# z2 of a gated MLP by one level of Strassen on blocks of 256 columns, on one NeuronCore

## The chip, the core and the metric

The kernel runs on one core of a Trainium2 chip. The metric is device time in microseconds (us) of one execution. The engines are PE (TensorE, matmuls), DVE (VectorE), ACT (ScalarE), POOL (GpSimd) and SP (SyncE, which here issues every DMA).

## The reference, cut to what matters

```python
xn = _layernorm(x)                                   # x: 2048 tokens x 576
s  = A(xn)                                           # sliding-window attention, 32 heads of 18, then @ wo
z  = _gelu(xn @ w_in)                                # 2048 x 4608
z1, z2 = z[..., :2304], _layernorm(z[..., 2304:])
g  = einsum("ts,bsf->btf", w_sp, z2) + b_sp[None, :, None]     # w_sp: 2048 x 2048
out = x + s * _silu((z1 * g) @ w_out)
```

The change is in the product `xn @ w_in[:, 2304:]`, called the z2 projection: 2048 x 576 times 576 x 2304, with gelu and the statistics of the layer norm behind it. All matrix products are done in fp32 by splitting each operand into a high part (fp32r) and a low part: three matmuls, high x high, high x low and low x high.

## The kernel before

The stages follow one another: statistics and transposes of x with the q/k projection, the values projection, the z2 projection, attention with the z1 projection filling its gaps, the output projection of attention, the product with w_sp (by Strassen with seven products, from sums of its quarters that were written to DRAM earlier), and the product with w_out (also by Strassen).

From the first stage on, the normalised x lies transposed in SBUF as 18 planes (`plane`, L192): nine groups of 64 inputs, high parts in planes 0 to 8, low parts in 9 to 17. A plane is 128 partitions by 1024 columns; partitions 0 to 63 hold one half of the tokens, 64 to 127 the other. A matmul on the upper and one on the lower 64 rows (`h` = 0, 1) run as a pair on PE; `steps_on` (L204) issues 27 such pairs for one token tile of 128 per half: nine planes by three matmuls.

The values stage (L942 to L957) makes two halves of 288 columns by eight token tiles `q`; each tile is evicted by ACT into `ve` and stored to v_d.

The z2 stage (L965 to L1002) makes six pieces of 384 columns by eight token tiles. For each tile: 27 pairs, gelu from PSUM by ACT (L991), `bn_stats` by DVE (L992), and after every second tile a store to z2_d (L994). The weights of the next piece are fetched by SP and halved by ACT and DVE (`split`, L117) meanwhile (`load_z2`, L906). In the last piece the first heads of attention are loaded (`pair_jobs`, L539) and 32 score maxima are put between the matmuls (`max_item`, L606).

Beside the z2 stage, `sp_combos` (L864) makes the sums of w_sp's quarters that the product with w_sp needs later: 16 rounds, each of four loads of 128x512 (256 KB), four GpSimd sums and four stores to sc_d. It is a generator: after each token tile the loop calls `next(combos)` once (L983), and a round takes three of these calls. Its four tiles a11, a12, a21, a22 come from the pool `wc` with `WCB` = 2 buffers each, and a round's loads are issued before the stores of the round before.

In this part of the kernel the order of the instructions of each engine, SP included, is the program's order (`manual_schedule`). SP waits for what a DMA needs (data to be stored, or a buffer whose earlier users, stores among them, are done) before it goes on to the next DMA. PSUM has eight banks; `pair_banks` gives the projections two pairs of them in turn.

## Time and profile before

| | us |
|---|---|
| median of three runs | 1827.39 (1827.34 to 1832.03) |
| the profiled execution | 1826.5 |
| its span, first to last instruction | 1824.4 |

A profile shows one execution. Its page has busy times by engine, the chain of work that ended last, and the costliest groups of instructions by line; windows give the same by stretches of time, and a timeline gives single instructions with what they waited for. Times are us from the start of the span unless marked ns. L209 is line 209 of the kernel before. A matmul's listed duration is its latency; matmuls overlap, so the distance between the starts of two of them tells the rate.

### The profile page before, as it was taken

Reading aid. Unit: us, or ns where it says so; the run is one execution under the profiler, and the core shown is the slowest. Engines: PE = TensorE matmul, PEld = TensorE weight load, DVE = VectorE, ACT = ScalarE, POOL = GpSimd, SP = SyncE. Lnnn points to the kernel's source line nnn. Section 1 sums busy time; section 2 is a strip of 40 time slices with the busy share of each in tenths; the row PEclk is TensorE's granted clock in tenths of the full one; section 3 lists DMA queues with packets and bytes.
Section 4 is the critical chain, followed back from the end, with each engine's and each line's share of the span. In section 5 each row is a group of like instructions: output and inputs, shape, how many; then the busy total and the mean of one; then the engine's idle time right before and its main releaser. Section 6 shows DMA issues by size and latency. Waiting matters only on the chain.

```text
span 1824.4 us, 37719 instructions
## 1 busy us (share of the span) xinstructions
PE 1798.9 (99%) x14373; PEld 1589.3 (87%) x14373; DVE 1129.3 (62%) x2314; ACT 931.9 (51%) x1742; POOL 427.7 (23%) x507
## 2 busy tenths in 40 slices
PE   8999999999999999999999999999999999999998
PEld 8999999998887887886988888888888888899998
DVE  7321333457676776671257687677876667767876
ACT  5433222222766666766467665466454534444443
POOL 3332333343455655645000000113000000000000
PEclk9999999999999999999999999999999999999999
DMA  8895688887567777765877768798786556797554
GB/s 275 194 231 168 226 278 283 279 269 240 162 167 205 197 185 195 202 166 167 266 236 251 236 214 282 242 300 298 233 284 233 178 176 200 255 264 205 159 156 137
DMA packets 266918, 405.73 MB, mean 222 GB/s; under 512 B 52337, under 2 KB 180593, under 8 KB 266609
## 3 DMA queue, kind: packets, MB, share of 16 engines
q1 hardware_dynamic: 266736, 403.32, 72.3%
q8 instruction: 113, 1.85, 0.4%
q14 instruction: 69, 0.56, 0.1%
HBM read 285.35 MB, written 117.09 MB: 221 GB/s over the span
## 4 chain that ended last, share of the span: by engine, by line
PE 83%; DMA 7%; DVE 5%; ACT 2%; SPq 2%; issue 1%; POOL 0%; ACTq 0%; DVEq 0%; POOLq 0%
PE acc L1498 35%; PE mb L209 11%; PE c L1590 8%; PE ma L209 5%; PE s L696 5%; PE ops L784 4%; PE t L696 3%; PE wops L1217 3%; PE ma L696 2%; PE mb L696 1%; SPq L366 1%; PE s L619 1%; DMA wraw<-in_w_qk_dram 1%; PE s L755 1%; DMA st_d<-qkhl 1%
## 5 line engine op out<-in xcount | busy, mean ns | idle before, releaser
L1498 PE MATMUL acc<-spl,zh 128*128 128x512 f32 x1008 | 392.6, 390 | 0.9 <-DVE spl L119 0.6
L1498 PE MATMUL acc<-sph,zl 128*128 128x512 f32 x1008 | 392.2, 389 | 0.0
L1498 PE MATMUL acc<-sph,zh 128*128 128x512 f32 x1008 | 392.2, 389 | 0.0
L119 DVE TENSOR_TENSOR spl<-spr,sph 128x1024 fp32r<-128x1024 f32 x168 | 210.3, 1252 | 39.5 <-ACT sph L118 37.9
L1498 PEld LDWEIGHTS acc<-spl,zh 128*128 128x128 f32 x1008 | 189.2, 188 | 41.7 <-DVE spl L119 2.6
L1498 PEld LDWEIGHTS acc<-sph,zh 128*128 128x128 f32 x1008 | 189.2, 188 | 39.4
L1498 PEld LDWEIGHTS acc<-sph,zl 128*128 128x128 f32 x1008 | 189.2, 188 | 39.1
L118 ACT ACTIVATE zh<-b 128x384 fp32r<-128x384 f32 x168 | 87.4, 520 | 209.7 <-PE acc L1498 209.4
L118 ACT ACTIVATE sph<-spr 128x1024 fp32r<-128x1024 f32 x168 | 176.0, 1047 | 14.0 <-DMA spr<-in_w_sp_dram 6.4
L119 DVE TENSOR_TENSOR zl<-b,zh 128x384 fp32r<-128x384 f32 x168 | 98.8, 588 | 123.3 <-ACT zh L118 123.2
L623 DVE CUSTOM_DVE_ANT_0 s<-s,band 128x384 f32<-128x384 f32 (+2 forms) x244 | 130.6, 559 | 46.7 <-PE s L619 24.2
L696 PE MATMUL s<-b,z1wh 64*128 64x512 f32 x522 | 155.1, 396 | 0.0
L1590 PE MATMUL c<-b,o 128*128 128x288 f32 x1056 | 144.1, 295 | 1.7 <-DVE o L119 1.7
L1590 PEld LDWEIGHTS c<-b,o 128*128 128x128 f32 x1056 | 141.0, 188 | 2.7 <-DVE o L119 2.4
L759 ACT ACTIVATE pt<-s 128x384 f32<-128x384 f32 (+2 forms) x257 | 111.1, 453 | 43.4 <-PE s L755 30.8
L992 DVE BATCH_NORM_STATS2 st<-zt 128x6 f32<-128x384 f32 x96 | 49.3, 548 | 129.8 <-ACT zt L991 129.4
L696 PE MATMUL t<-b,z1wh 64*128 64x512 f32 x378 | 123.7, 397 | 0.2 <-ACT z1o L706 0.2
L209 PE MATMUL ma<-z2w,b 64*128 64x384 f32 x648 | 116.1, 333 | 0.0
L209 PE MATMUL mb<-z2w,b 64*128 64x384 f32 x648 | 116.0, 333 | 0.0
L209 PE MATMUL ma<-att,b 64*128 64x384 f32 x648 | 112.8, 331 | 0.0
L209 PE MATMUL mb<-att,b 64*128 64x384 f32 x648 | 112.8, 331 | 0.0
L209 PEld LDWEIGHTS mb<-z2w,b 64*128 64x128 f32 x648 | 112.4, 184 | 0.0
(264 smaller groups left out, 4781.9 us busy)
## 6 DMA issues: line engine op xcount, KB each, us to landing
spr<-sc_d SPq DMA_DIRECT2D x96, 512.0 KB
spr<-in_w_sp_dram SPq DMA_DIRECT2D x72, 512.0 KB
zr<-z_d SPq DMA_DIRECT2D x144, 192.0 KB
z_d<-zt SPq DMA_DIRECT2D x48, 384.0 KB
z_d<-z1o SPq DMA_DIRECT2D x72, 256.0 KB
z1t<-z_d SPq DMA_DIRECT2D x72, 256.0 KB
y_d<-z1t SPq DMA_DIRECT2D x72, 256.0 KB
a<-in_w_sp_dram SPq DMA_DIRECT2D x64, 256.0 KB
```

Source lines behind the costliest of these rows:

```text
L118: act.activation(hi, src, AF.Copy)
L119: dve.tensor_tensor(lo, src, f32(hi), ALU.subtract)
L209: pe.matmul(banks[h][:, :n], *both[h][i], start=i == 0, stop=i == STEPS - 1)
L366: sp.dma_start(rows[c].rearrange("i h a p -> (i h) a p"), f32(hl[64 * n:64 * n + 64, c]).rearrange("q (a p) -> q a p", a=2))
L623: dve.tensor_tensor_reduce(out=ps[:, :w], in0=ps[:, :w], in1=band[:, m0:384], scale=1.0, scalar=-3.0e38, op0=ALU.add, op1=ALU.max, accum_o ...
L696: pe.matmul(ps, w, x_, start=n == 0, stop=n == STEPS - 1)
L759: act.activation(pt[:, j, d0:d0 + n * P], ps[:, (qa - a) * P:(qa - a + n) * P], AF.Exp, scale=scale)
L784: pe.matmul(o_ps[c][32 * j:32 * j + 32, (qa - 4 * c) * P:(hi - 4 * c + 1) * P], vgs[u][:, kb - k0, j * VW:j * VW + 32], pt[:, j, (qa - kb) ...
L992: dve.bn_stats(st2[:, s, pc, :], zv)
L1217: pe.matmul(po[:, i, :288], lt[:, cs], r[:, i * 288:(i + 1) * 288], start=n == 0, stop=n == len(pl) - 1)
L1498: pe.matmul(acc[j], z[:, ps], w[:, cs], start=s == i == 0 and n in OPENS, stop=s == 7 and i == 2, skip_group_check=True)
L1590: pe.matmul(banks[key][:, :288], y, w, start=begin and k == n == 0, stop=close and k == 8 and n == 2, skip_group_check=True)
```

## The change

The z2 projection is cut into nine blocks of 256 columns (`ZB`, `NZ`). Eight of them are made in four pairs by one level of Strassen (the form with seven products and shared sums): the tokens in two halves of 512 columns of a plane, the inputs in planes 0 to 3 and 4 to 7, the columns in the two blocks of the pair. Plane 8, the ninth, is no part of the Strassen scheme; its products are added to four of the seven as further steps, with activations from plane 8 itself or the difference of its two token halves (`xdd`). The ninth block is made the plain way.

- The sums of activations (`x_sums`) are made by DVE and ACT during the values stage, one step after each token tile. A fourth operand, the difference of the token halves of planes 0 to 3, is written over the second halves of these planes during the first two products (`third_sum`); what stood there is saved to x_d before and brought back by DMA at the end (`restore`).
- The sums of weights T1 to T4 are made by GpSimd (`form_t`) for each pair of blocks from half blocks that SP fetches (`fetch_w`, `fetch_rem`) during the pair before.
- Each of the seven products is two groups `qq` of two token tiles, into four PSUM banks of its kind; `evict` copies it, adds it to an earlier one, or applies gelu. Finished outputs go through `closed`: gelu, statistics and the store, which are issued after the next group (`run_behind`). The output tiles `zt_tile` come in turn from two pools, seven in all.
- `sp_combos` has one buffer for each tile instead of two, and its loads, sums and stores stand at three successive calls of `next(combos)`. There is one call after each group.
- The head loads stand ahead of the groups of the last pair's fourth to sixth product, the maxima in its seventh and in the ninth block.

The diff, cut to its core:

```diff
-                wc = open_pool(stack, "wc", bufs=WCB)
+                wc = open_pool(stack, "wc", bufs=1)
+                for q, h in ((q, h) for q in range(8) for h in range(2)):
...
+                        sp.dma_start(t, w_sp[i, 8 * j + q, :, cs])
...
                     yield
                     pool.tensor_tensor(a22, a21, a22, ALU.add)
                     pool.tensor_tensor(a21, a11, a21, ALU.subtract)
-                    yield
                     pool.tensor_tensor(a11, a22, a11, ALU.subtract)
                     pool.tensor_tensor(a12, a12, a11, ALU.subtract)
-                    if n + 1 < len(steps):
-                        nxt = load(*steps[n + 1])
                     yield
                     for k, t in enumerate((a22, a11, a21, a12)):
                         sp.dma_start(sc_d[k, q, :, cs], t)
+                    yield
...
+                LEFT = (own(8, 0), own(8, 512), summed(xdd))
+                PARTS = [(own(0, 0), 0, True, None), (own(4, 0), 1, True, (0, 0)), (summed(xs2), 0, False, None),
+                         (summed(xs1), 1, True, (1, 1)), (own(0, 512), 0, False, None),
+                         (own(4, 512), 0, False, (1, 0)), (summed(xs4), 1, False, (2, 1))]
...
+                def x_sums():
...
+                    for i, k0 in ((0, 0), (1, 4)):
+                        sp.dma_start(raw[i], w_z2[0, :, k0:k0 + 4, :])
+                    for i in range(2):
+                        for k in range(4):
+                            sp.dma_start(x_d[i, :, k], f32(half_plane(9 * i + k, 1)))
+                    for k in range(4):
...
+                        dve.tensor_tensor(s, f32(h21), f32(h22), ALU.add)
+                        dve.tensor_tensor(s, s, f32(l21), ALU.add)
+                        dve.tensor_tensor(s, s, f32(l22), ALU.add)
+                        split(xs1[0][:, c], xs1[1][:, c], s)
+                        yield
+                        less(s, h11, l11)
+                        split(xs2[0][:, c], xs2[1][:, c], s)
+                        yield
+                        dve.tensor_tensor(s, f32(h12), s, ALU.subtract)
+                        dve.tensor_tensor(s, s, f32(l12), ALU.add)
+                        split(xs4[0][:, c], xs4[1][:, c], s)
+                        yield
...
-                        if ch == 1 or q >= 6:
-                            next(nxt[1], None)
+                        next(forming, None)
...
+                def fetch_w(key, blk, k0, name):
...
+                    sp.dma_start(t, w_z2[blk, :, k0:k0 + 4, :])
+                def halve_rem(n):
+                    split(rem[:, 0, :n], rem[:, 1, :n], raw_w["rem"][:, :n])
+                def form_t(*names):
+                    b11, b12, b21, b22 = (raw_w[n] for n in ("b11", "b12", "b21", "b22"))
+                    for n in names:
+                        dst, x_, y = {"t3": (b12, b22, b12), "t2": (b11, b12, b11), "t4": (b21, b21, b11),
+                                      "t1": (b11, b22, b11)}[n]
+                        pool.tensor_tensor(dst, x_, y, ALU.add if n == "t2" else ALU.subtract)
+                def group_steps(banks, qq, operands, opens, ends):
+                    for a in range(2):
...
+                        for xo, j, wt in operands:
+                            for xi, wi in ((0, 0), (0, 1), (1, 0)):
+                                for h in range(2):
+                                    pe.matmul(banks[h][:, cs], xo(xi, j, q)[ROWS[h]], wt[ROWS[h], wi],
...
...
+                def evict(n, qq, banks, blks):
+                    for h in range(2):
+                        i, b = 2 * qq + h, banks[h]
+                        if n in (0, 2, 4):
+                            act.activation((u2 if n == 2 else t1)[:, i], b, AF.Copy)
+                        elif n == 1:
+                            zv = zt_tile()
+                            dve.tensor_tensor(zv, b, t1[:, i], ALU.add)
+                        elif n == 5:
+                            zv = zt_tile()
+                            act.activation(zv, b, AF.Gelu_apprx_tanh)
+                        elif n == 6:
+                            zv = zt_tile()
+                            dve.tensor_tensor(zv, b, u2[:, i], ALU.add)
+                        if n == 4:
+                            zv = zt_tile()
+                            dve.tensor_tensor(zv, yb[qq][h], t1[:, i], ALU.add)
...
+                    run_behind()
...
+                for p in range(NP):
...
+                    def prepare(n):
+                        if n == 0:
+                            halve_rem(2)
+                            ops_w[2] = halve(raw_w["b11"])
+                            form_t("t4", "t1")
+                        elif n < 5:
+                            ops_w[n + 2] = halve(raw_w[("b11", "b12", "b21", "b22")[n - 1]])
+                        elif n == 5:
+                            ops_w[7] = halve(raw_w["b11"])
+                        else:
+                            if not final:
+                                form_t("t3", "t2")
+                            ops_w[8] = halve(raw_w["b21"])
+                    def fetches(n):
...
+                        if n == 5 and not final:
+                            fetch_w("b22", nxt + 1, 4, "z1wl")
+                        if n == 6:
+                            fetch_rem((nxt,) if final else (nxt, nxt + 1))
+                    for n, (xo, kind, opens, part_of) in enumerate(PARTS):
...
+                        for qq in range(2):
+                            banks = (xb, yb)[kind][qq]
+                            if qq == 0:
+                                prepare(n)
+                            if final and n > 2:
+                                if qq == 0 and n < 6:
+                                    clear(n - 3)
+                                    heads_in += [job for job in [pair_jobs(n - 3)] for _ in range(8)]
+                                unasked(4)
+                            for m, _ in enumerate(group_steps(banks, qq, operands, opens, n > 4)):
+                                if final and n == 6:
+                                    more_maxima(m)
+                            evict(n, qq, banks, blks)
+                            if qq == 1:
+                                fetches(n)
+                            if p == 0 and n < 2:
+                                third_sum(2 * n + qq)
+                            if final and n in (5, 6):
+                                restore(2 * (n - 5) + qq)
+                            next(combos, None)
...
+                halve_rem(1)
...
+                for qq in range(4):
...
+                    unasked(4)
+                    for m, _ in enumerate(group_steps(banks, qq, operands, True, True)):
+                        more_maxima(m)
+                    next(combos, None)
+                    run_behind()
```

More of the change, by code (lines that the diff above doesn't have):

```diff
@@ L101 @@
     t_d = dram.tile([4, FB, 288], F32, name="t_d")
+    x_d = dram.tile([2, P, 4, 512], F32, name="x_d")
     ident = const.tile([P, P], F32, name="ident")
@@ L874, in load @@
                         ts.append(t)
-                    return ts
-                nxt = load(*steps[0])
-                for n, (q, cs) in enumerate(steps):
-                    a11, a12, a21, a22 = nxt
+                    a11, a12, a21, a22 = ts
                     yield
@@ L932, in token_tile, with difference @@
+                def difference(s, k):
+                    h0, l0, h1, l1 = (half_plane(9 * i + k, t) for t in range(2) for i in range(2))
+                    dve.tensor_tensor(s, f32(h0), f32(h1), ALU.subtract)
+                    dve.tensor_tensor(s, s, f32(l0), ALU.add)
+                    less(s, l1)
+                ops_w = {}
                 def token_tile(q, h):
@@ new lines, in unasked, with more_maxima @@
+                def unasked(n):
+                    for _ in range(n):
+                        if heads_in:
+                            next(heads_in.pop(0), None)
+                def more_maxima(count):
+                    if count % 6 == 3 and ahead:
+                        max_item(0, *ahead.pop(0))
+                fetch_w("b11", 0, 0, "z1wh")
+                fetch_w("b12", 1, 0, "z1wl")
+                fetch_w("b22", 1, 4, "z1wl")
+                fetch_w("b21", 0, 4, "z1wh")
+                fetch_rem((0, 1))
```

210 lines of the change are left out of this document (135 added, 75 removed).

## The prediction

> **What bounds the kernel now.** I read the page first (busy shares, the chain that ended last), then the line of the projection matmuls, then the z2 stage on each engine and on SP's queue.
>
> ```profile
> span 1824.4 us, 37719 instructions
> PE 1798.9 (99%) x14373; PEld 1589.3 (87%) x14373; DVE 1129.3 (62%) x2314; ACT 931.9 (51%) x1742; POOL 427.7 (23%) x507
> ...
> PE 83%; DMA 7%; DVE 5%; ACT 2%; SPq 2%; issue 1%; POOL 0%; ACTq 0%; DVEq 0%; POOLq 0%
> ```
>
> PE is busy for 99% of the span and 83% of the chain. So less matmul work is worth its whole time, as long as nothing else then ends last in that stage.
>
> ```profile
> L209 PE MATMUL ma<-att,b x648: 331/331/339, 194.8 to 381.8; 64*128 64x384 f32 x162
> L209 PE MATMUL mb<-z2w,b x648: 330/333/443, 232.3 to 423.9; 64*128 64x384 f32 x162
> ```
>
> ```profile
> 136.40:166.00 29.60, 29.06 (x433) 28.60 (x431) 1.34 (x2) 7.13 (x17) 8.10 (x19) 1.00 0.66 178
> 166.00:194.70 28.70, 28.70 (x438) 28.70 (x436) 4.52 (x9) 9.41 (x25) 5.48 (x15) 1.00 0.39 130
> 231.90:269.00 37.10, 37.10 (x432) 37.10 (x430) 15.71 (x25) 10.71 (x25) 10.93 (x8) 1.00 0.86 284
> ```
>
> The z2 stage runs from 194.7 to 424.0: 229.3 us. The window rows (columns: length, then PE, PEld, DVE, ACT, POOL busy with counts, clock, DMA share, GB/s) show two values windows and one whole z2 piece. In the piece PE never stops, the granted clock is 1.00, but the DMA engines are already busy for 0.86 of the time at 284 GB/s.
>
> **Part one: the matmuls.** Two matmuls, one for each half of the rows, run as a pair.
>
> ```profile
> 45.92 0.28 PE L383 MATMUL ma<-b,wqh 64*128 64x256 f32 x1
> ...
> 46.49 0.27 PE L383 MATMUL ma<-b,wqh 64*128 64x256 f32 x1
> ```
>
> ```profile
> 239.67 0.33 PE L209 MATMUL ma<-z2w,b 64*128 64x384 f32 x1
> ...
> 241.92 0.33 PE L209 MATMUL ma<-z2w,b 64*128 64x384 f32 x1
> ```
>
> Five pairs of 256 columns take 0.57 us: 0.114 each (I take 0.116); thirteen of 384 take 2.25: 0.173. Before: 6 pieces x 8 token tiles x 27 = 1296 pairs, 224.7 us. After: one pair of blocks has 7 products x 4 token tiles x 12 steps, and 4 of the products carry 3 more steps for the ninth plane: 336 + 48 = 384 pairs. Four such are 1536; the ninth block adds 8 x 27 = 216. In all 1752 x 0.116 = 203 us. **PE is relieved of about 21 us.** The 32 maxima stay (229.3 - 224.7 = 4.6 us of the stage).
>
> **Part two: the elementwise work.**
>
> ```profile
> L1447 DVE TENSOR_TENSOR cb<-acc,t 128x512 f32<-128x512 f32 x36 | 23.7, 689 | 5.8 <-PE acc L1498 5.8
> L992 DVE BATCH_NORM_STATS2 st<-zt 128x6 f32<-128x384 f32 x96 | 49.3, 548 | 129.8 <-ACT zt L991 129.4
> L119 DVE TENSOR_TENSOR spl<-spr,sph 128x1024 fp32r<-128x1024 f32 x168 | 210.3, 1252 | 39.5 <-ACT sph L118 37.9 <-DMA z1t<-z_d 1.2 <-DMA s_d<-so 0.4
> L118 ACT ACTIVATE sph<-spr 128x1024 fp32r<-128x1024 f32 x168 | 176.0, 1047 | 14.0 <-DMA spr<-in_w_sp_dram 6.4 <-DMA spr<-sc_d 5.6 <-DVE spl L119 1.9
> L1423 ACT ACTIVATE z1t<-z1t 128x512 f32<-128x512 f32 x72 | 43.3, 625 | 41.9 <-DMA z1t<-z_d 41.0
> L275 POOL TENSOR_TENSOR wql<-wraw,wqh 128x1152 fp32r<-128x1152 f32 x13 | 35.0, 2703 | 57.7 <-ACT wqh L272 46.8 <-DVE xpair L323 9.6 <-ACT qkhl L118 1.3
> ```
>
> For two blocks (384 x 0.116 = 44.5 us of PE): DVE has 12 sums from PSUM at 0.69, 32 statistics of 256 columns at about 0.4 (0.548 scaled down), 7 halvings at 1.25: 30 us. ACT has 28 copies and gelus at 0.62 and 7 halvings at 1.05: 25 us. GpSimd has 4 weight sums of 128x1024 at about 2.4 (2.70 scaled): 10 us. These lie beside PE. In the values stage the activation sums are some 44 DVE operations of 512 columns at 0.69 plus two halvings, 33 us, where DVE was busy for 5.9 of 58 us; they cost nothing there. Their eight stores to x_d and two weight loads go ahead of the value stores on SP, at most 10 x 0.5 = 5 us if nothing covered them; I take 0.
>
> **Part three: the combinations of w_sp.** Their arithmetic is unchanged, but the four tiles go from two buffers to one, and a round (four loads, four GpSimd sums, four stores) is spread over three groups of matmuls. A group lasts 24 or 30 pairs, so a round is due every 3 x 44.5 / 14 = 9.5 us; before it was due every 3 x 27 x 0.173 = 14.0.
>
> ```profile
> 203.61 1.29 POOL L881 TENSOR_TENSOR a<-a,a 128x512 f32<-128x512 f32 x1 [12.42 <-DMA a<-in_w_sp_dram]
> 204.98 1.29 POOL L882 TENSOR_TENSOR a<-a,a 128x512 f32<-128x512 f32 x1
> 206.35 1.28 POOL L884 TENSOR_TENSOR a<-a,a 128x512 f32<-128x512 f32 x1
> 207.71 1.30 POOL L885 TENSOR_TENSOR a<-a,a 128x512 f32<-128x512 f32 x1
> 213.40 1.29 POOL L881 TENSOR_TENSOR a<-a,a 128x512 f32<-128x512 f32 x1 [4.39 <-DMA a<-in_w_sp_dram]
> ...
> 217.71 1.49 POOL L885 TENSOR_TENSOR a<-a,a 128x512 f32<-128x512 f32 x1
> 223.72 1.30 POOL L881 TENSOR_TENSOR a<-a,a 128x512 f32<-128x512 f32 x1 [4.53 <-DMA a<-in_w_sp_dram]
> ...
> 298.13 1.29 POOL L881 TENSOR_TENSOR a<-a,a 128x512 f32<-128x512 f32 x1 [11.93 <-DMA a<-in_w_sp_dram]
> ```
>
> ```profile
> 196.34 1.84 SPq L873 DMA_DIRECT2D a<-in_w_sp_dram  x4
> ...
> 205.80 2.62 SPq L873 DMA_DIRECT2D a<-in_w_sp_dram  x4
> ...
> 215.48 3.70 SPq L873 DMA_DIRECT2D a<-in_w_sp_dram  x4
> ...
> 252.64 3.23 SPq L890 DMA_DIRECT2D sc_d<-a  x4
> ...
> 290.07 3.06 SPq L873 DMA_DIRECT2D a<-in_w_sp_dram  x4
> ...
> 384.25 8.19 SPq L552 DMA_DIRECT2D att<-st_d  x16
> ```
>
> The four sums take 203.61 to 209.01: 5.4 us. From the end of the last load's issue to the first sum I read 5.4 (198.18 to 203.61), 5.0, 4.5 (219.18 to 223.72) and 5.0 (293.13 to 298.13). The stores' landing has no row of its own. Its nearest rows:
>
> ```profile
> DMA  9999999999999898953220060000000000000000
> ```
>
> ```profile
> 188.18 0.40 ACT L954 ACTIVATE ve<-mb 128x288 f32<-128x288 f32 x1
> ```
>
> ```profile
> 190.83 0.36 POOL L953 MEMSET ve<- 128x320 f32 x1 [0.25 <-DMA v_d<-ve]
> ```
>
> The DMA row covers 256 to 260 us in slices of 0.1: traffic ends at 258.4, 2.5 us after the last sc_d issue ended (255.87). The smaller value store was out 2.25 us after its data was written, issue included (188.58 to 190.83).
>
> With one buffer these add up in a ring: sums 5.4, issue of the last store 0.5, its landing 2.7, then the loads of a12, a21 and a22 (a12 waits for that store, the other two stand behind it on SP) 1.4, then 4.6 until the data is there, since the traffic is thinner than before: **R = 14.6 us a round, where 9.5 is due**. By the lowest rows it is 5.4 + 2.25 + 0.9 + 4.5 = 13.1; with GpSimd's sums slowed to 1.57 each (the 1.49 row and its gap) and the landings at 3.2 and 5.4, 16.5.
>
> At one place a page speaks against the change: the Trainium skill, "Trainium Kernel Development and Optimization", Best Practices, says to double-buffer so that DMA overlaps compute; the old two-buffer round of 14.0 us with PE never stopped agrees.
>
> **Why this reaches PE.** SP issues in program order and holds everything behind a waiting DMA: the weights of the next two blocks (w_z2's half blocks and the ninth plane), the z2 stores that free the seven output tiles, the head loads. The ninth plane's weights are fetched after the last product of a pair, and its halving stands ahead of all evictions on ACT; the next pair's second product needs it. So PE can be only some groups ahead of SP, and SP walks at R. The stage then is:
> - 18 us until the first w_sp sums: six z2 weight loads (2.4 MB, about 10 us at 284 GB/s with 2 us to start) go first, then GpSimd forms T3, T2, T4, T1, 4 x 2.4 us, ahead of them in its order, the first while the last loads land;
> - 15 R = 219 to the last round's sums; 4.5 for two rounds in which weight sums stand in GpSimd's order ahead of sums whose data is there;
> - 6 for the last sums and stores;
> - 22 on SP: 24 head loads, 10 z2 stores, 6 restores, 1 weight load at 0.51 each (8.19 / 16) until the last ninth-plane fetch, which moved behind the head loads;
> - 4.5 for its landing and halving;
> - 27 for the ninth block beyond the steps that do not need it (25 - 2.8) and the maxima.
>
> Sum 82 + 15 R = **301 us** against 229.3: +72. Before, PE hid all of this; now its 21 us come out as idle, with some 70 more. Span 1824.4 + 72 = 1896; the profiled execution took 1826.5 (2.1 around the span) and the median is 0.9 above it: **1899 us**.
>
> **The rivals.**
> - *The round trip is hidden* (faster). If PE could run far enough ahead, or a round trip took less than (229.3 - 82) / 15 = 9.8 us, the saving stays: 1827.4 - 21 = 1806. Against it: sums 5.4 and load landing 4.5 alone make 9.9. For it: in windows without z2 stores SP could catch up. Chance 0.12.
> - *A shorter round.* The Trainium skill, "DMA: Bandwidth & Descriptors", Anatomy of one DMA, gives about 2 us plus bytes over 436 GB/s (measured there on GpSimd's path), 2.6 us for 256 KB; the rows of 4.5 to 5.4 disagree as long as other traffic is in front. As a mechanism of this kernel: with PE slowed, the DMA queues are nearly empty when a load comes, and the landing falls to that of the lone stores (2.5); R = 5.4 + 0.5 + 2.5 + 1.4 + 2.5 = 12.3, stage 266, 1864. Chance 0.12.
> - *DVE and GpSimd in each other's way.*
>
> ```profile
> L119 DVE TENSOR_TENSOR z2w<-z1wh,z2w x18: 540/552/1655, 215.2 to 375.2; 128x384 fp32r<-128x384 f32 x18
> ```
>
> A halving of 0.55 us took up to 1.66 while GpSimd's sums ran. If most of the 28 halvings and the early sums meet GpSimd so, R passes 16.5 and the time 1928; point of decision: GpSimd busy for over half of the stage. Chance 0.08. (The Trainium skill, "SBUF — State Buffer", two separate sides, calls the shared port an exclusive lock for a whole instruction; both engines slowing, 1.29 to 1.49 and 0.55 to 1.66, agree in part.)
> - That fewer columns don't save PE time is excluded as far as the 256-column row goes; it is that very shape.
>
> **How the numbers follow.** Forecast 0.68, with R from 13.1 to 16.5: 1876 to 1927. The shorter round adds 1864, so the range is 1855 to 1927; the hidden round trip (0.12) and the port case (0.08) stay outside. About 0.3% (5.5 us) is what a measurement of this kernel can tell from no change. Faster 0.13 (the first rival and a little), within 0.03, slower 0.84.
>
> **What would show it.** Right: w_sp sums starting 13 to 16.5 us apart after the first pair of blocks; loads of a12 on SP waiting for sc_d stores in nearly every round; PE idle of 60 to 100 us between 195 and 500, ended by the halving of the ninth plane or of T2, in gaps once per pair of blocks; PE's busy time down by about 20. Wrong: rounds 9.5 us apart with PE unbroken (the first rival), or gaps ended by DVE sums of the products rather than by fetched weights.

## The result and the profile after

The changed kernel takes **1936.7 us** (median of four runs, 1929.62 to 1943.06) against 1827.37 for the kernel before on the same chip: a ratio of **1.0591** (95% interval 1.0549 to 1.0632), 109 us slower. The forecast was 1899 us with a range to 1927. The profiled execution took 1935.0 us.

The page after: busy time of the engines, and PE and its granted clock in 40 slices.

```profile
span 1933.3 us, 39916 instructions
PE 1810.0 (94%) x15285; PEld 1587.6 (82%) x15285; DVE 1211.9 (63%) x2451; ACT 975.5 (50%) x1764; POOL 476.2 (25%) x523
...
PE   8999768567799999999999999999999999999999
PEclk9999889778899999999999999999999999999999
```

The dents of PE and of its clock lie in the fifth to eleventh slices (193 to 532 us), the last of the values stage and the z2 stage; the gap of the values stage is too short to show in a slice. Behind them the stages take their old time: z1 starts 108.4 us later (532.3 against 423.9), and the span is 108.9 us longer.

One row for the whole z2 stage before, then windows after: the whole z2 stage, the stretch of the values stage that has the gap, then z2 up to the first sum of w_sp's quarters, up to the first sum of the last round, and the rest.

```profile
194.80:423.90 229.10, 228.90 (x2626) 227.43 (x2626) 108.52 (x219) 62.87 (x145) 89.07 (x68) 1.00 0.84 277
```

```profile
202.00:532.30 330.30, 238.00 (x3541) 231.82 (x3537) 162.81 (x318) 99.88 (x162) 137.69 (x83) 0.84 0.64 208
...
136.40:166.00 29.60, 23.65 (x311) 22.71 (x309) 15.16 (x23) 9.25 (x19) 6.90 (x16) 0.88 0.77 225
...
202.00:222.10 20.10, 13.90 (x195) 13.40 (x191) 7.05 (x4) 3.37 (x6) 10.02 (x4) 0.83 0.53 187
222.10:463.10 241.00, 177.38 (x2695) 173.04 (x2693) 117.35 (x193) 83.86 (x133) 118.35 (x73) 0.84 0.66 219
463.10:532.30 69.20, 46.72 (x661) 45.38 (x658) 38.41 (x123) 12.65 (x23) 9.32 (x7) 0.83 0.57 177
```

The stage takes 330.3 us instead of 229.1. PE idles for 92.3 of them (330.3 - 238.0; before 0.2). Its busy time did not fall by the some 21 us of saved matmuls but rose by 9.1, because the granted clock was 0.84 in the mean of the stage, idle time included, and not 1.00 (the last section tells why). As an account: 92.1 more idle, plus 9.1 more busy, is the 101.2 by which the stage grew, and the values stage adds 7.2 (z2 starts at 202.0 instead of 194.8).

Why PE idles is seen in three views of one place. First PE and ACT at the start of the second pair of blocks (the bracket tells the idle time before an instruction and what ended it):

```profile
294.33 0.58 PE L1039 MATMUL ma<-zrem,b 64*128 64x256 f32 x1 [13.28 <-ACT zrem L120]
```

```profile
293.64 0.63 ACT L120 ACTIVATE zrem<-z1raw 128x512 fp32r<-128x512 f32 x1 [14.60 <-DMA z1raw<-in_w_z_dram]
```

Then SP's queue ahead of it:

```profile
278.28 4.39 SPq L884 DMA_DIRECT2D sc_d<-a  x4
...
283.81 2.12 SPq L874 DMA_DIRECT2D a<-in_w_sp_dram  x4
...
286.96 1.98 SPq L1018 DMA_DIRECT2D z1raw<-in_w_z_dram  x2
```

PE waits 13.3 us for the ninth plane's halved weights, ACT 14.6 for their DMA, and SP issued that DMA at 286.96, after it had gone through a whole round of w_sp. The waits of SP from 200 to 500, added up, say on whom (columns: us in total, times, longest):

```profile
SPq L884 <- POOL a L878: 63.7, 15, 13.3
SPq L884 <- POOL a L880: 41.4, 15, 3.3
...
SPq L874 <- DMA sc_d<-a: 9.6, 11, 1.9
```

The stores to sc_d (L884) wait for GpSimd's sums 15 times, the loads (L874) for those stores. That is the ring. A turn of it stands in the chain of waits, late in the stage:

```profile
437.68 2.04 DMA sc_d<-a
...
440.74 5.77 DMA a<-in_w_sp_dram
446.67 1.28 POOL a L878
...
451.64 2.39 POOL a L881
454.05 2.04 DMA sc_d<-a
```

From landing store to landing store it is 16.4 us (437.68 to 454.05): store 2.0, issues 1.0, load 5.8, sums 7.4. Not every turn is this bare: the chain begins at 406.6 in this stage, and in the two rounds before (to 437.7) it leaves a w_sp store for two loads of z2 weights and a T sum on GpSimd, behind which the w_sp sums stand. The first sums of the rounds on GpSimd:

```profile
222.14 1.73 POOL L878 TENSOR_TENSOR a<-a,a 128x512 f32<-128x512 f32 x1
...
246.46 1.29 POOL L878 TENSOR_TENSOR a<-a,a 128x512 f32<-128x512 f32 x1 [17.49 <-DMA a<-in_w_sp_dram]
...
463.14 1.29 POOL L878 TENSOR_TENSOR a<-a,a 128x512 f32<-128x512 f32 x1 [9.12 <-DMA a<-in_w_sp_dram]
```

Between the second (246.46) and the sixteenth (463.14) lie 14 rounds of 15.5 us, where 9.5 was due; the first took 24.3.

### The profile page after: what moved, and what is told of

It reads as the page before. It is cut to its first block, busy times and chain, and to the rows that moved or that the text cites. A ratio compares the mean times of both kernels' runs of the same rounds, so it can differ in the third digit from the quotient of the medians.

```text
span 1933.3 us, 39916 instructions
## 1 busy us (share of the span) xinstructions
PE 1810.0 (94%) x15285; PEld 1587.6 (82%) x15285; DVE 1211.9 (63%) x2451; ACT 975.5 (50%) x1764; POOL 476.2 (25%) x523
## 3 DMA queue, kind: packets, MB, share of 16 engines
q1 hardware_dynamic: 277152, 408.56, 69.2%
## 4 chain that ended last, share of the span: by engine, by line
PE 66%; DMA 6%; DVE 3%; POOL 1%; issue 1%; ACT 1%; SPq 0%; POOLq 0%; DVEq 0%; ACTq 0%
PE acc L1704 34%; PE c L1796 8%; PE s L698 5%; PE ops L786 4%; PE t L698 3%; PE wops L1423 3%; PE mb L698 2%; PE ma L698 2%; PE s L621 1%; PE s L757 1%; DMA y_d<-z1t 1%; DMA att<-st_d 1%; PE t L621 1%; DMA z1wh<-in_w_z_dram 1%; DMA a<-in_w_sp_dram 1%
## 5 line engine op out<-in xcount | busy, mean ns | idle before, releaser
L770 POOL TENSOR_SCALAR_AFFINE_SELECT pt<-pt 128x512 f32<-128x512 f32 x128 | 81.4, 637 | 121.2 <-ACT pt L761 118.8
L621 PE MATMUL s<-att 54*128 54x384 f32 (+1 forms) x244 | 82.4, 357 | 23.4 <-DVE mx L625 12.9
L1511 POOL TENSOR_TENSOR o<-o 128x576 f32<-128x576 f32 (+1 forms) x5 | 7.2, 1431 | 392.6 <-DMA o<-in_w_out_dram 392.6
L698 PE MATMUL s<-b,z1wl 64*128 64x512 f32 x261 | 94.3, 395 | 0.4 <-POOL z1wl L1208 0.4
L625 DVE CUSTOM_DVE_ANT_0 t<-t,band 128x384 f32<-128x384 f32 (+2 forms) x136 | 75.7, 569 | 29.5 <-PE t L621 14.1
L698 PEld LDWEIGHTS s<-b,z1wh 64*128 64x128 f32 x522 | 86.1, 186 | 5.2 <-ACT z1wh L1208 1.7
```

The source lines that it names most:

```text
L621: pe.matmul(ps[:, :w], q_of(u, j)[0:54, i * P:(i + 1) * P], k_of(u, j)[0:54, k0:k0 + w], start=True, stop=True)
L625: dve.tensor_tensor_reduce(out=ps[:, :w], in0=ps[:, :w], in1=band[:, m0:384], scale=1.0, scalar=-3.0e38, op0=ALU.add, op1=ALU.max, accum_o ...
L698: pe.matmul(ps, w, x_, start=n == 0, stop=n == STEPS - 1)
L770: pool.affine_select(out=pt[:, :, 0:P], in_=pt[:, :, 0:P], pattern=[[0, 4], [1, P]], compare_op=ALU.is_ge, fill=0.0, base=0, channel_multi ...
```

## The experiments

The theory: the w_sp combinations, in one buffer on SP's in-order queue, set the pace of the stage. The rivals: the bytes are too many for the DMA engines in the shorter stage; GpSimd's sums and DVE are in each other's way; or the new z2 scheme itself loses time. Ratios are against the kernel before, with 95% intervals.

**The combinations taken apart.** Three kernels made from the one after; the sums S1 to S4 are read from w_sp itself where sc_d isn't written.

e_no_sums (no combinations at all):

```diff
-                combos = sp_combos(gate)
+                combos = iter(())
```

> Left out: the sums of w_sp's quarters, with their loads and stores (the later product loads quarters of w_sp in their place, the same sizes). Theory (the one-buffer round trip of loads, sums and stores on SP's in-order queue holds PE): PE runs through the z2 stage but for its start and the head loads, 203 us of pairs + 5 of maxima + about 10, and the values stage keeps its 7 us; total about 1823 us (1812 to 1835). Rivals (GpSimd's and DVE's load; the bytes to be moved in a shorter stage) expect the same, since both are gone; this run says what all three together cost.

Measured: 1844.35 us, 1.0081 (1.0054 to 1.0109). So 93 of the 109 us belong to the combinations; but the time is 9 us above the upper end of what was expected, and the new z2 isn't faster even without them.

e_sums_only (GpSimd's 64 sums, without loads and stores):

```diff
-                        sp.dma_start(t, w_sp[i, 8 * j + q, :, cs])
...
-                    for k, t in enumerate((a22, a11, a21, a12)):
-                        sp.dma_start(sc_d[k, q, :, cs], t)
```

> Left out: the loads and stores of w_sp's quarters; GpSimd still makes the 64 sums of 128x512, at the same places of its order, on tiles filled once with zeros. Theory (round trip on SP): within 8 us of the run without any sums, since nothing waits for a DMA. Rival (GpSimd's sums and DVE in each other's way): still above 1900 us, most of the 109 us kept.

Measured: 1865.33 us, 1.0192 (1.0168 to 1.0217), 21 us above e_no_sums: between theory and rival. The sums alone do cost. With nothing to wait for they crowd into the start, and there the timeline shows DVE's third sums slowed (L956 and L957 make the first two of their three steps):

```profile
222.15 0.68 DVE L956 TENSOR_TENSOR z1o<-b 128x512 f32<-128x512 f32 x1
222.87 2.78 DVE L957 TENSOR_TENSOR z1o<-z1o,b 128x512 f32<-128x512 f32 x1
...
230.61 1.67 DVE L957 TENSOR_TENSOR z1o<-z1o,b 128x512 f32<-128x512 f32 x1
```

GpSimd suffers as well (1.29 us a sum alone, 1.59 to 2.13 here). A DVE sum of 0.68 takes 1.67 beside GpSimd's 512-column sums and 2.78 beside a T sum of 1024 columns.

e_moves_only (loads and stores in one buffer, without the sums):

```diff
-                    pool.tensor_tensor(a22, a21, a22, ALU.add)
-                    pool.tensor_tensor(a21, a11, a21, ALU.subtract)
-                    pool.tensor_tensor(a11, a22, a11, ALU.subtract)
-                    pool.tensor_tensor(a12, a12, a11, ALU.subtract)
```

> The changed kernel with one buffer; left out: GpSimd's sums, so that the loaded quarters are stored as they are. All loads and stores and their places stay. Theory (the ring of sums, store, landing, load, landing on SP): a round falls by the 5.4 to 6.5 us of the sums from 15.5 to about 9.5, as often as rounds are due, so PE is held little: 1850 to 1870 us. Rival (bytes): the bytes are the same, so the time stays above 1900 (most of what two buffers left).

Measured: 1894.7 us, 1.0356 (1.0327 to 1.0386): above the theory's range and just short of the rival's. The rounds on SP, from issue to issue of the loads:

```profile
302.72 3.17 SPq L874 DMA_DIRECT2D a<-in_w_sp_dram  x4
...
310.37 2.28 SPq L880 DMA_DIRECT2D sc_d<-a  x4
...
313.46 3.40 SPq L874 DMA_DIRECT2D a<-in_w_sp_dram  x4
...
326.05 3.19 SPq L874 DMA_DIRECT2D a<-in_w_sp_dram  x4
```

The sums were 5.4 to 7.4 us of a turn, but without them it is only 3 to 5 shorter (10.7 and 12.6 here): 4.5 us pass from the last load's issue (305.89) to the stores, and the loads now take over 3 us to issue; SP waits 21 times for a store to sc_d before a load, 24 us in all from 205 to 440. The DMA engines are busy for 0.89 of the time between 300 and 350, at 300 GB/s. The parts of a ring can't be taken off one by one at their price.

**One buffer or two.** e_before_one_buffer is the kernel before with the generator of the kernel after (one buffer); e_two_buffers is the kernel after with the old generator. Two buffers don't fit there beside three buffers of halved weights, so these go to two, and the weights are halved one product later:

```diff
-                wc = open_pool(stack, "wc", bufs=1)
+                wc = open_pool(stack, "wc", bufs=WCB)
...
-                    return ga.tile([P, 2, 4, ZB], F32R, name="zwop", bufs=3)
+                    return ga.tile([P, 2, 4, ZB], F32R, name="zwop", bufs=2)
```

> The kernel before with only the pool of w_sp's tiles cut to one buffer and the generator as in the change. Theory: a round takes about 15.5 us where 14.0 is due, and SP falls behind by 15 x 1.5 = 22 us over the stage: 1840 to 1855 us. If the two rivals (load of GpSimd and DVE, bytes in a shorter stage) were the whole cause, nothing changes here: 1827.

> The changed kernel with the generator and the two buffers of before; room is made by two instead of three buffers for the halved weights, which are halved one product ahead instead of two. Theory: rounds come at 9.5 to 11 us, PE mostly unbroken, about 1835 us (1820 to 1855). Rival load of GpSimd and DVE: the sums are all still there, above 1900. Rival bytes: 16 rounds and the rest are 56 MB in the first 3.4 pairs of blocks, at 300 GB/s 187 us instead of 153, so about 1857.

Measured: e_before_one_buffer 1853.73 us, 1.0117 (1.0098 to 1.0137), as expected: one buffer costs 21 us even where a round has 14.0 us. The first sums of its first and fourteenth round:

```profile
202.59 1.29 POOL L876 TENSOR_TENSOR a<-a,a 128x512 f32<-128x512 f32 x1 [11.43 <-DMA a<-in_w_sp_dram]
...
404.36 1.26 POOL L876 TENSOR_TENSOR a<-a,a 128x512 f32<-128x512 f32 x1 [5.92 <-DMA att<-st_d]
```

These 13 rounds take 15.5 us each, as in the kernel after, though 14.0 were due here and 9.5 there: the ring has a pace of its own. e_two_buffers 1899.78 us, 1.0372 (1.0347 to 1.0397): 40 us come back, not the 82 to 117 expected. Between 300 and 350 the DMA engines are now busy for 0.92 of the time, at 304 GB/s. Two kernels tell apart what is left: e_two_buffers_moves is e_two_buffers without the sums, e_no_sums_two_halved is e_two_buffers without any combinations.

> e_two_buffers without the 64 sums of the combinations (left out; their loads and stores are kept). Theory: with two buffers the loads and stores no longer wait for each other, and what is left of the cost are GpSimd's sums (21 us by themselves) and the waits behind them; without them the time is 1848 to 1866, ratio 1.010 to 1.020. Rival: the bytes are the limit (share 0.92 at 304 GB/s), so it stays at 1880 to 1900, ratio 1.028 to 1.038.

> e_two_buffers without the w_sp combinations (sums, loads and stores left out); the weights are still halved one product later into two buffers. If the missing third buffer is what e_two_buffers and e_two_buffers_moves paid for, the five gaps of 5 to 8 us stay and the time is near e_two_buffers_moves: 1875 to 1890, ratio 1.025 to 1.033. If the loads and stores are (bytes, SP's queue), the gaps go and the time is near e_no_sums: 1840 to 1852, ratio 1.006 to 1.013. I hold the second for a little likelier, since the ninth plane's fetch then finds an idle queue.

Measured: 1885.38 us, 1.0310 (1.0293 to 1.0327), the rival's range; and 1857.49 us, 1.0157 (1.0130 to 1.0184), between the two expectations. The windows from 300 to 350, with the moves and without:

```profile
300.00:350.00 50.00, 41.78 (x672) 41.29 (x672) 23.48 (x43) 19.30 (x30) 9.48 (x4) 0.90 0.91 304
```

```profile
300.00:350.00 50.00, 49.75 (x850) 49.55 (x848) 29.75 (x56) 25.26 (x42) 9.62 (x4) 1.00 0.42 133
```

So, taken off in this order, with two buffers the displaced third buffer of halved weights costs 14 us (1.0157 against 1.0081), the loads and stores 28, the sums 11. With one buffer there are no such separate prices: 93 us in all.

| ratio to before | no sums | with GpSimd's sums |
|---|---|---|
| no loads and stores | 1.0081 | 1.0192 |
| no loads and stores, two halved-weight buffers | 1.0157 | not run |
| two w_sp buffers, two halved-weight buffers | 1.0310 | 1.0372 |
| one w_sp buffer | 1.0356 | 1.0591 |

**Two buffers of half the size.** e_half_tiles keeps the three buffers of halved weights, and makes 32 rounds on tiles of 256 columns in two buffers (with the mend of the values stage, below); e_half_tiles_dve also makes the T sums on DVE and fetches the ninth plane after the second product.

```diff
-                wc = open_pool(stack, "wc", bufs=1)
+                wc = open_pool(stack, "wc", bufs=2)
+                steps = [(q, slice(h * 256, h * 256 + 256)) for q in range(8) for h in range(4)]
...
+                    t = wc.tile([P, 4, 256], F32, name="a")
```

> The kernel after with the mend of the values stage and with the combinations in 32 rounds on tiles of 256 columns, so that two buffers stand in the memory of one and the three buffers of halved weights stay; two loads and one store a round. The bytes are the same. Theory: the one-buffer ring on SP's queue is what the combinations cost, and the two-buffer kernels so far paid for their missing third buffer of halved weights; then the gaps of 12 to 13 us before the ninth plane go, and the time is 1846 to 1873, ratio 1.010 to 1.024. Rival: the bytes (0.9 of the DMA engines) hold it in any arrangement: 1883 to 1900, ratio 1.030 or more.

> e_half_tiles with the four T sums of z2's weights on VectorE and the ninth plane fetched after the second product. Theory: GpSimd's order and the late fetch are what is left beside the start of z2, so 5 to 15 us below e_half_tiles, at best near e_no_sums_values (ratio 1.005). Rival: VectorE, which has the halvings, the sums from PSUM and the statistics too, becomes the engine that TensorE waits for, and the time is the same as or above e_half_tiles.

Measured: 1918.56 us, 1.0506 (1.0480 to 1.0531), and 1900.47 us, 1.0400 (1.0372 to 1.0427). Both expectations fall for the first: it regains nothing beside the mend it contains (1.0521, below), and the DMA engines are less busy than with whole tiles, so the bytes don't hold it (0.79 of the time at 229 GB/s between 300 and 350). SP's and GpSimd's rows tell why:

```profile
296.36 0.89 SPq L874 DMA_DIRECT2D a<-in_w_sp_dram  x2
297.41 0.37 SPq L890 DMA_DIRECT2D sc_d<-a  x1
...
304.54 0.89 SPq L874 DMA_DIRECT2D a<-in_w_sp_dram  x2
```

```profile
303.45 0.74 POOL L883 TENSOR_TENSOR a<-a 128x256 f32<-128x256 f32 x1 [7.04 <-DMA a<-in_w_sp_dram]
...
309.49 0.74 POOL L883 TENSOR_TENSOR a<-a 128x256 f32<-128x256 f32 x1 [1.88 <-DMA a<-in_w_sp_dram]
```

The loads issued by 297.25 and 305.43 are there 6.2 and 4.1 us later, though a round loads half as much, two transfers of 256 KB and not four (whole tiles: 4.5 to 5.8), and the load of 304.54, which needs the buffer of the store of 297.41, came 7.1 us after it. A half tile waits about as long as a whole one, so two half buffers turn no faster than one whole buffer: some 8 us for half the work. The second kernel's 18 us come from GpSimd's order or the ninth plane's fetch; which, wasn't parted.

**The values stage.** In the kernel after, PE's gap there is ended by ACT's eviction of `ve`:

```profile
148.07 0.60 PE L211 MATMUL ma<-wvh,b 64*128 64x288 f32 x1 [4.68 <-ACT ve L988]
```

Two theories, two half mends: e_spread_saves gives the x_d saves two to a plane; e_late_first_sum forms the first sum one group later.

```diff
-                    for i in range(2):
-                        for k in range(4):
-                            sp.dma_start(x_d[i, :, k], f32(half_plane(9 * i + k, 1)))
                     for k in range(4):
+                        for i in range(2):
+                            sp.dma_start(x_d[i, :, k], f32(half_plane(9 * i + k, 1)))
```

> The changed kernel with one edit: the eight stores to x_d are issued two at a time beside the sums of each plane instead of all at the first token tile of the values stage. Theory: the 5 us gap of PE at 143 us, its echo and the half clock after it go, the rest stays: 5 to 8 us less, about 1930 us. Rival (the gap comes from the sums' DVE and ACT work or from the q/k stores): no difference, 1937.

> The kernel after, with the first activation sum formed one group of the values stage later (the two weight loads and the eight x_d saves stay where they are). Theory: TensorE's 5.0 us gap at 143.1 comes from ScalarE, whose rounding of the first sum waits 8.3 us for the last st_d store of qkhl, with the evictions of ve queued behind it; with the sum one group later there is no gap at 143, z2 starts at 195 to 198 instead of 202.0, and the time falls to 1928 to 1932. Rival: the two loads and the eight saves on SP hold back the stores of v_d and so the ve buffers; then a gap of 4 to 5 us stays near 145, z2 starts at 201 to 202, and the time stays at 1934 to 1938.

Measured: 1931.68 us, 1.0562 (1.0535 to 1.0589), and 1934.98 us, 1.0585 (1.0562 to 1.0609). Neither mends it. The first lies inside its theory's range, but its interval overlaps that of the kernel after, a gap of 4.5 us stays, and z2 starts at 202.1; in the other z2 starts at 206.7. In the second, ACT's and SP's rows show two waits one behind the other:

```profile
149.95 0.63 ACT L120 ACTIVATE att<-t 128x512 fp32r<-128x512 f32 x1 [6.61 <-DMA st_d<-qkhl]
...
161.73 0.41 ACT L989 ACTIVATE ve<-ma 128x288 f32<-128x288 f32 x1 [8.26 <-POOL ve L988]
```

```profile
135.10 12.66 SPq L368 DMA_DIRECT2D st_d<-qkhl  x16
...
148.93 5.70 SPq L932 DMA_DIRECT2D x_d<-b  x8
155.39 49.70 SPq L992 DMA_DIRECT2D v_d<-ve  x30
```

The first rounded sum waits for the last st_d stores, with the evictions behind it on ACT; and the value stores stand on SP behind st_d, two loads and eight saves until 155.39, so that the four `ve` buffers run out. e_values_mended removes both: it begins three groups later, with the saves two to a plane. e_no_sums_values is that without combinations.

```diff
+                    for _ in range(3):
+                        yield
```

> The kernel after, with the activation sums, their two weight loads and the x_d saves begun three groups of the values stage later, the saves spread two to a plane. Theory now: two waits stand one behind the other there, ScalarE's rounding that waits for the last st_d store, and the first v_d stores that stand on SP behind the st_d stores, the two loads and the eight saves (6.7 us), so that the four ve buffers run out; either mend alone only moves the gap. With both gone there is no gap of TensorE over 2 us between 136 and 195, z2 starts at 195 to 198 instead of 202.0, and the time falls to 1927 to 1932. Rival: the DMA engines themselves are the limit there (their share was 0.77 between 136 and 166): a gap of 4 us or more stays, z2 starts at 200 or later, and the time stays at 1933 to 1938.

> Leaves out the w_sp sums with their loads and stores, as e_no_sums did, with the same mend of the values stage. Theory: the values stage cost e_no_sums 7 to 8 us, so 1834 to 1840, still not faster than the kernel before: the rest is the start of z2, whose first weights can only be loaded when the values stage is over. Rival: the values stage was hidden by what came after it, and the time stays at 1842 to 1848.

Measured: 1926.1 us, 1.0521 (1.0491 to 1.0551), and 1838.92 us, 1.0052 (1.0036 to 1.0067): the first 1 us below its range, the second inside it. The gap is gone, and z2 starts at 193.7:

```profile
136.40:166.00 29.60, 28.89 (x433) 28.45 (x431) 13.87 (x21) 10.72 (x24) 7.82 (x19) 1.00 0.77 217
```

**The fetch of the ninth plane, and all mends together.** e_early_ninth fetches it after the second product instead of the last; e_no_sums_mended leaves the combinations out and mends the order at the start.

```diff
-                        if n == 6:
+                        if n == 1:
                             fetch_rem((nxt,) if final else (nxt, nxt + 1))
```

> The changed kernel with one edit: the ninth plane's weights for the next pair of blocks are fetched after the second product instead of the seventh. Theory (SP walks at the pace of the rounds, and the ninth plane is only the place where PE notices): the gaps before the ninth plane's steps go, others come (T2, output tiles), rounds stay at 15 to 16 us, and only the end of the stage, where that fetch stood behind the head loads, gains: 1915 to 1930 us. Rival (the late fetch is itself the cause; ACT waited 58 us for it, PE 40): about 1895.

> Leaves out the w_sp sums with their loads and stores, as e_no_sums did, and adds four moves: the first activation sum one group later, the ninth plane fetched after the second product and first of all in the first pair of blocks, the third sums one product later. Theory: what e_no_sums still lost beside the 21 us that TensorE saves is the values stage (7 us) and the start of z2 (about 9 us with the half clock behind it); with both mended the time is 1820 to 1832, so the products alone gain at most a few us over the kernel before. Rival: the losses sit in the half clock and in the evictions of every pair, and the time stays at 1836 to 1844.

Measured: 1930.89 us, 1.0553 (1.0525 to 1.0581): PE's waits for the ninth plane's halving fell from 44 us to 14, and others came, ended by evictions. Behind those stand other weights and output tiles (ACT waits 48.8 us for T sums, 12.9 in the kernel after), and the rounds stayed at 15 us. And 1842.45 us, 1.0082 (1.0057 to 1.0107), the rival's: it had only the half mend of the values stage, and a gap of 7 us came back there.

e_all_mended has two w_sp buffers, the early fetch, spread saves, later third sums and the rounds spread over 50 of 60 groups. e_mended_dve adds the whole mend of the values stage and the T sums on DVE; e_no_sums_mended_dve is that without combinations.

```diff
-                        pool.tensor_tensor(dst, x_, y, ALU.add if n == "t2" else ALU.subtract)
+                        dve.tensor_tensor(dst, x_, y, ALU.add if n == "t2" else ALU.subtract)
```

> Two buffers, early fetch of the ninth plane (for the first pair too), spread saves, third sums one product later, and the rounds spread over 50 of the stage's 60 groups. Theory: rounds are due every 11.5 us and two buffers carry that; what is left is the bytes, some 64 MB in the stage, at 300 GB/s 213 us, just the length that PE needs: 1820 to 1845 us. Rival (GpSimd and DVE in each other's way beyond what the run with the sums alone showed, 21 us): 1850 to 1880.

> e_all_mended with the activation sums begun three groups later (the mend of the values stage) and the four T sums of z2's weights on VectorE instead of GpSimd. Theory: e_all_mended stood at ratio 1.0285 with gaps of 11.2, 7.2 and 8.5 us that end by weights whose T sums stand behind w_sp sums in GpSimd's order; with these sums on VectorE and the 7 us of the values stage gone the time is 1838 to 1856, ratio 1.005 to 1.015. Rival: the bytes hold it (share 0.9 between 300 and 350), and only the values stage's 7 us go: 1866 to 1878.

> e_mended_dve without the w_sp combinations (sums, loads and stores left out). e_mended_dve stood at 1.0279. If its gaps of 4 to 8 us before the second product come from the two buffers for the halved weights, they stay, at ratio 1.015 to 1.025; if they come from the combinations, 1.000 to 1.008.

Measured: 1880.77 us, 1.0285 (1.0253 to 1.0317), just above the rival's range; 1879.95 us, 1.0279 (1.0252 to 1.0306), above both ranges; 1840.12 us, 1.0062 (1.0037 to 1.0086), the range of the combinations. The T sums on GpSimd were not what held the mended kernel. The combinations still cost 40 us there (1.0279 against 1.0062), as in e_two_buffers (39). No version tried beats the kernel before.

## Why the prediction was right in kind and short in size

**The matmuls: right.** In the stage after, 56 matmuls of 256 columns stand in one row:

```profile
317.77 3.48 PE L1039 MATMUL s<-zwop,b 64*128 64x256 f32 x56
```

Less the last one's latency of 0.28, that is 3.2 us for some 27.5 pairs, 0.116 a pair, as forecast. On the other side 1296 pairs at 0.173 are 224.2 us, not 224.7, and by the piece shown in the prediction (37.1 us for 216 pairs, 0.172 each) a little less, so 19 to 21 us are saved; without combinations and with the values stage mended they are spent again inside z2, as the stage's row of e_no_sums_values shows:

```profile
195.90:432.50 236.60, 218.84 (x3541) 215.80 (x3537) 157.40 (x320) 100.42 (x163) 43.54 (x19) 0.96 0.47 149
```

PE idles 17.8 us in it, nearly all at the start, where by the program the first weights can't be loaded before the values stage frees their memory (another place for them was not tried), and at the end; and its busy time is about 11 above the 208 that full clock would give (228.9 - 21), at a clock of 0.96.

**The ring: right, and the step that failed by its size.** SP did walk at the pace of the ring, and nearly half of PE's idle time was of the kind foretold: 44 of the 92 us were ended by the ninth plane's halving. But 14 were ended by DVE's sums of the products, which the prediction had named as a sign of being wrong, 11 by ACT's evictions, and 21 lay late in the stage, before the maxima. The stage was forecast as 18 + 15R + 4.5 + 6 + 22 + 4.5 + 27 with R = 14.6:

| term | forecast | measured |
|---|---|---|
| values stage | 0 | 7.2 |
| z2 start to first w_sp sums | 18 | 20.1 |
| 15 rounds, with collisions | 219 + 4.5 | 241.0 |
| last round's sums to z1 | 6 + 22 + 4.5 + 27 = 59.5 | 69.2 |

The failed step is this sum's 82 us beside the rounds, together with the 0 for the values stage: they were taken as fixed, and the range was made by R alone. The rounds' pace came out at 15.5, inside the stated 13.1 to 16.5. Of the 36.5 us that the two stages took beyond the forecast, 7.8 are that pace; the other 28.7 are the values stage (7.2), the start (2.1), a wait in the first round (9.7) and the end (9.7). In the rounds: 14 of them at 15.5 are 7.8 us above 14 of 14.6 with their share of the collisions (216.7 against 204.4 + 4.5 = 208.9), and the first, at 24.3, is 9.7 above. Its cause is a wait that the sum did not have. SP, in the first round:

```profile
223.90 5.42 SPq L884 DMA_DIRECT2D sc_d<-a  x4
239.00 0.90 SPq L1056 DMA_DIRECT2D z_d<-zt  x2
239.99 1.95 SPq L874 DMA_DIRECT2D a<-in_w_sp_dram  x4
```

SP stands from 229.3 to 239.0 for z2's first stores, whose gelu on ACT stands behind the third sums. GpSimd's w_sp sums slow these on DVE, but that is the smaller part. In e_no_sums, which has no w_sp sums, SP's first z2 stores are these:

```profile
237.17 6.94 SPq L1056 DMA_DIRECT2D z_d<-zt  x3
```

They come 33.8 us after the start of its z2 stage (203.4), here 37.0 after 202.0. So some 3 us are the slowing, and the rest is when the first outputs are ready at all.

In the turn shown, the sums (7.4 against 5.4) and the load (5.8 with its issue, against 4.6 without) were longer, the store (2.0 against 2.7) and the issues shorter. Redone from its own terms the upper R is 16.8 and not 16.5, which makes 1932 us and still falls short; for the store landing of 3.2 in it the prediction gives no row, and the stores in the chain took 2.0.

**"They cost nothing there" (activation sums): wrong by 7.2 us.** DVE did have the time. The cost came through ACT and SP, where a wait for a store holds what stands behind it. The prediction had counted the ten DMAs and taken 0 of the 5 us; it hadn't asked what memory the rounded sums go to.

**"6 + 22 + 4.5 + 27": 9.7 short.** SP issued the last ninth-plane fetch at 496.37, 33.2 us after the last round's sums began (28 forecast, of which the 41 DMAs at 0.51 are 21 and not 22). Its landing and halving took 6.3 (4.5), until 502.7, and the ninth block 29.6 (27).

**"PE's busy time down by about 20": wrong.** It rose by 9.1 in the stage, at a clock of 0.84. How much of the time this cost can't be read from it: while SP sets the pace, a slower matmul only fills idle time.

**The rivals.** The hidden round trip fell. The shorter round fell too: the landing of a load didn't shrink with thinner traffic (5.8 us in the chain). The Trainium skill, "DMA: Bandwidth & Descriptors", Anatomy of one DMA, would have given an estimate of about 2.6 us for one such load by itself; the loads of a round come four at a time, and none in these rows comes near that. DVE and GpSimd in each other's way was no rival but a part of the result: 21 us in e_sums_only, and some 3 us of the first round here. GpSimd was busy for 0.42 of the stage (137.7 of 330.3), below the half that the prediction had set as the point of decision. The advice of the Trainium skill ("Trainium Kernel Development and Optimization", Best Practices) to double-buffer agrees with the runs: the second buffer was worth 40 us here, net of the third buffer of halved weights that it displaced, and 21 in the kernel before.

**Still open:** what of the 28 us that loads and stores cost with two buffers is the bytes and what is SP's order. The after-stage moves 68.7 MB (330.3 us at 208 GB/s); at 304 GB/s, the highest of the 50 us windows looked at, these take 226 us, more than the 208 that PE needs. But short stretches went faster (393 GB/s over 4.5 us, in the last section), so no ceiling is shown, and neither is that the bytes hold the mended kernels, at 0.8 to 0.9 of the DMA engines. The ring no longer does: in e_mended_dve SP waits from 200 to 440 for z2's gelus 70 us and for stores to sc_d only 8.

## What to carry to other kernels

When a stage gets shorter, ask first whether what runs beside it still fits: its bytes over the highest rate seen, and the turn of its buffer over the new period. A load, a sum and a store in one buffer form a ring whose parts add up and trade with each other; smaller tiles don't help where landing hardly depends on size. And where one queue issues everything in order, a wait of one transfer is paid by the transfers behind it, so count what stands there before taking away a buffer.

## What the runs showed of the hardware that wasn't expected

- After a gap PE ran at half the clock for some us. Windows of the kernel after, from the end of the gap in the values stage on:

```profile
148.10:152.30 4.20, 4.20 (x33) 4.18 (x35) 3.31 (x6) 1.45 (x4) 0.00 (x0) 0.50 0.97 326
152.50:157.00 4.50, 4.50 (x72) 4.50 (x70) 3.03 (x5) 0.63 (x1) 0.00 (x0) 1.00 1.06 393
```

  The gap of 4.7 us (the bracket at 148.07 above) and the half of 4.2 us make 6.8 of the 7.2 us of that stage. The Trainium skill, "TensorE: Matmul & The Clock Gate", Part 1, states such a gate, which closes to half after an idle window of about 3.4 us and opens after a busy one; the rows agree. In the z2 stage it is the same, here after the gap of 13.3 us:

```profile
294.30:299.20 4.90, 3.63 (x30) 3.34 (x32) 4.89 (x5) 3.91 (x7) 4.82 (x3) 0.50 0.32 109
```

  The forecast had counted every gap at its length alone.
- A DVE sum of 0.68 us took 1.67 beside GpSimd's sums and 2.78 beside a larger one (e_sums_only); GpSimd's own went from 1.29 to between 1.6 and 2.4. The times look like turns taken: the DVE sum of 222.87 ended at 225.65, just over half a us after GpSimd's T sum (222.37 to 225.09).
- Landing hardly depended on a load's size. In the chain of waits of the kernel after, where a piece of a DMA runs from its issue to its landing, z1wl is a load of 512 KB and z1raw one of 128 KB:

```profile
421.04 5.15 DMA z1wl<-in_w_z_dram
...
496.37 5.39 DMA z1raw<-in_w_z_dram
```

  The load of 256 KB shown before took 5.8 us (440.74), while the stores of 256 KB beside it took 2.0.
